# Spectral mixing and gated MLP in one kernel: two rows of x asked for ahead of a DFT block, and a row's statistics ahead of a low part on VectorE

## The chip, the cores and the metric

The kernel runs on one core of a Trainium2 chip. The metric is the device time of one execution in microseconds (us), here the median over several runs. The engines are TensorE (PE; PEld for its weight loads), VectorE (DVE), ScalarE (ACT), GpSimd (POOL) and SyncE (SP). Each takes its instructions in the order in which the program lists them for that engine. SP issues nearly all loads of the part that matters here.

## The reference

x has 2048 rows of 512 numbers. A first half mixes it by Fourier matrices, a second half is a gated MLP with a matrix over the sequence. Both are added to x, and six vectors (from a small product with `c`) scale, shift and gate them.

```python
def _A_ref(x, dft_seq_re, dft_seq_im, dft_hid_re, dft_hid_im):
    a = jnp.einsum("bsd,ed->bse", x, dft_hid_re)
    b = jnp.einsum("bsd,ed->bse", x, dft_hid_im)
    return jnp.einsum("ts,bse->bte", dft_seq_re, a) - jnp.einsum("ts,bse->bte", dft_seq_im, b)

def _B_ref(x, w_in, w_sp, b_sp, w_out):
    z = _gelu(jnp.einsum("bsd,df->bsf", x, w_in))
    z1 = z[..., :Fh]
    z2 = _layernorm(z[..., Fh:], axis=-1)
    g = jnp.einsum("ts,bsf->btf", w_sp, z2) + b_sp[None, :, None]
    return jnp.einsum("bsf,fd->bsd", z1 * g, w_out)

mod = (_silu(c) @ w_mod).reshape(c.shape[0], 6, 1, -1)
sa, ca, ga, sb, cb, gb = (mod[:, 0], mod[:, 1], mod[:, 2], mod[:, 3], mod[:, 4], mod[:, 5])
h = _layernorm(x, axis=-1) * (1 + ca) + sa
x = x + ga * _A_ref(h, ...)
h = _layernorm(x, axis=-1) * (1 + cb) + sb
return x + gb * _B_ref(h, ...)
```

The change lies in the first 40 us of the first half: layer norm of x's rows, and the product of the sequence DFT matrices with them.

## The kernel before, in words

**Numbers in two parts.** All matrix products run in fp32r. Each operand is split into a high part (an fp32r copy, made on ScalarE) and a low part (the rest, a subtraction on VectorE), and a product is three matmuls: high with high, high with low, low with high (`matmul3`, L95 to L99).

**Tiles of the DFT matrices.** The sequence matrices come in blocks of 512 by 512 (`src`, real and imaginary in turn), 1 MB each, which SP loads with four DMAs of 256 KB into one of two `stage` buffers (`load_block`, L156). I call them block 0, 1, 2, and so on; the "fourth DFT block" of the change is block 3, an imaginary one. From a block VectorE makes four tiles of 128x512 by a transpose of 32x32 squares (L191, written to `t`). From `t`, ScalarE makes the high part `ah` (L268), and VectorE the low part `al` (L286). There are two buffers for `t`, four for `ah` and three for `al`. When the last tile of a block has been transposed, the load of the block two further on is put on SP (L269 to L272 in `prep_hi`, L478 to L480 in `turn_front`).

**Rows of x.** Row s, for s from 0 to 15, is here a set of 128 of the 2048 rows, with all 512 columns. Four rows together are one buffer `x`, of which there are two; a call of `load_x` (L422) loads some of the four with four DMAs. Rows 6 and 7 (the seventh and eighth) are 512 KB: four DMAs of 128 KB, each with 32 partitions for both rows. For rows 0 to 3, `stats_first` (L436) puts three small instructions on VectorE (L439, L441, L442) and two on GpSimd (L443, L444); ScalarE makes the high part `hh` (L491) and the normed row `xn` (L121), and VectorE the low part `hl` (L533, `lo_h`). For rows 4 to 9, `stats_x` (L433) puts L105 and L107 on VectorE and three small steps on GpSimd, then `norm_x` L121, `hi_h` L528 and `lo_h` L533 follow.

**Order of the work.** The order is written by hand, and each engine keeps it. First comes a list of calls, the head (from L1095), which prepares rows 0 to 3 and tiles 0 to 6. Then a loop runs over tiles n (L1277): `prep(n)` makes the high part of tile n+3 and the low part of tile n+2 where they don't exist yet; `mm_a(n)` puts the tile's twelve matmuls on TensorE; `run(n)` makes the calls that `at(n, ...)` has put down for this n. `FRONT` (L150) says that the first eight tiles are those of blocks 0 and 1, which are multiplied with rows 0 to 3 (L551 and L557). Tiles 8 to 11 are those of block 2, multiplied with rows 4 to 7; tiles 12 to 15 are those of block 3, again with rows 4 to 7; tiles 16 to 19 are those of block 4, with rows 8 to 11. From tile 8 on the matmuls are those of L97, L98 and L99: `ah` with `hh`, `al` with `hh`, `ah` with `hl`, four times per tile.

**What stands in the rows around the change.** Statistics of rows 4 and 5 are called at n = 4, their `hl` at n = 7. Statistics of rows 6 and 7 are called at n = 6 and so stand on VectorE ahead of tile 10's transpose, of tile 9's `al`, and of the `hl` of rows 4 and 5. In the program before, rows 6 and 7 are asked for at n = 0 (L1146), when the head has already put block 2 and block 3 on SP. The program gives SP's DMAs eight semaphores in turn, and each DMA waits until the eighth before it has landed. The first DMA of a block waits besides until the last transpose from its buffer is done.

Of the kernel before, what the change touches and what calls it, by code (L numbers as in the profile page):

```python
# [20 lines left out]
def fnet_gmlp_kernel(  # L21
# [98 lines left out]
    def apply(dst, src, scale_shift):  # L120
        nc.scalar.activation(dst, src, AF.Identity, bias=scale_shift[1], scale=scale_shift[0])  # L121
# [3 lines left out]
    def at(n, f, *a):  # L125
        fill.setdefault(n, []).append((f, a))
# [39 lines left out]
    def load(b):  # L166
        if b < len(src):
            stage[b] = blocks.tile([P, 16, P], F32, tag="stage", bufs=2, name=f"stage{b}")
            load_block(stage[b], src[b])
        elif b < len(src) + 2:  # L170
            j = b - len(src)
            XB.append(blocks.tile([P, 4, Q], F32, tag="stage", bufs=2, name=f"xb{j}"))
            for g in range(2):
                nc.sync.dma_start(XB[j][:, 2 * g:2 * g + 2], ht_d[g].rearrange("(k p) t -> p k t", p=P)[:, 2 * j:2 * j + 2])
                for kk in range(2):
                    TT[2 * j + kk, g] = XB[j][:, 2 * g + kk]
        elif 4 * (b - NB0) < NE - N4:
            i, gh = divmod(b - NB0, NQ)
            g, h = divmod(gh, 2)
            p = PROD[i]  # L180
            stage[b] = blocks.tile([P, 2, 16, 64], F32, tag="stage", bufs=2, name=f"stage{b}")
            for r in range(2):
                load_half(stage[b][:, r], s_d[S_OF[p], r, g] if p in S_OF else
                          quad(w_sp, r + (2 if p == 4 else 0), g + (2 if p == 1 else 0)), h)
# [5 lines left out]
    def squares(dst, block, k):  # L190
        nc.vector.transpose(dst.rearrange("p (b i) -> p b i", i=32), block[:, :, 32 * k:32 * k + 32])  # L191
# [10 lines left out]
    def slot(i, name, dtype=F32):  # L202
        return slots[0].tile([P, Q], dtype, tag=f"slot{i}", bufs=1, name=name)
# [19 lines left out]
    def form_t(n):  # L223

        if n < N1:
            gg, p, kk = (n - N2) // 4, (n - N2) // 2 % 2, n % 2
            return TT[2 * p + kk, gg]
        p = YPROD[(n - N1) // 4 % len(YPROD)]
        gg, kk = divmod(n % 4, 2)
        a, b, c, d = TT[kk, gg], TT[2 + kk, gg], TT[kk, 2 + gg], TT[2 + kk, 2 + gg]  # L230
        return {6: S2[gg, kk], 7: a if n < N3 else c, 4: b if n < N3 else d, 5: c if n < N3 else a, 3: d if n < N3 else b}[p]
# [21 lines left out]
    def prep_hi(n):  # L253
        if n >= NE or n in highs:
            return
        highs.add(n)
        if N2 <= n < N4:
            T[n] = form_t(n)
        else:
            b, k = FRONT[n] if n < len(FRONT) else divmod(n, 4) if n < N2 else (NB0 + (n - N4) // 4, (n - N4) % 4)  # L260
            if n not in T:
                T[n] = blocks.tile([P, Q], F32, tag="t", bufs=2, name=f"t{n}")
                if n >= N4:
                    squares(T[n], stage[b][:, k % 2], k // 2)
                else:
                    squares(T[n], stage[b], k)
        AH[n] = SE[2][:, n - N4] if N4 <= n < N4 + 4 else blocks.tile([P, Q], F32R, tag="ah", bufs=4, name=f"ah{n}")
        nc.scalar.activation(AH[n], T[n], AF.Copy)  # L268
        if not N2 <= n < N4 and k == 3 and b in stage:  # L269
            stage.pop(b)  # L270
            if b != NB0:
                load(b + 2)  # L272


    def prep_lo(n):
        if n >= NE or n in lows:
            return
        lows.add(n)
        if N2 <= n < N4 and n % 4 == 3:
            AL[n] = slot(0, f"al{n}", F32R) if slots else zrow[0].tile([P, Q], F32R, tag="z1u", bufs=6, name=f"al{n}")  # L280
        elif N4 <= n < N4 + 4:
            AL[n] = slot(9 + n - N4, f"al{n}", F32R)
        else:
            AL[n] = blocks.tile([P, Q], F32R, tag="al", bufs=3, name=f"al{n}")
        t = T.pop(n)
        nc.vector.tensor_tensor(AL[n], t, AH[n].bitcast(F32), op=ALU.subtract)  # L286
# [135 lines left out]
    def load_x(g, ks=range(4), eng=nc.sync):  # L422

        if g not in XG:
            XG[g] = spool.tile([P, 4, D], F32, tag="x", bufs=2, name=f"x{g}")
        k0, k1 = ks[0], ks[-1] + 1
        v = x.rearrange("(g a k i) d -> g a i k d", g=NQ, a=4, i=32)
        for a in range(4):
            eng.dma_start(XG[g][32 * a:32 * a + 32, k0:k1, :], v[g, a][:, k0:k1, :])
        for k in ks:  # L430
            X[4 * g + k] = XG[g][:, k, :]
# [4 lines left out]
    def stats_first(s):  # L436

        m = spool.tile([P, 12], F32, tag="first", bufs=4, name=f"first{s}")
        nc.vector.bn_stats(m[:, :6], X[s])  # L439
        mv = m[:, 8:]  # L440
        nc.vector.bn_aggr(mv[:, :2], m[:, :6])  # L441
        nc.vector.tensor_scalar(mv[:, 1:2], mv[:, 1:2], EPS, None, op0=ALU.add)  # L442
        nc.gpsimd.tensor_tensor(mv[:, 2:3], mv[:, 1:2], mhalf, op=ALU.pow)  # L443
        nc.gpsimd.tensor_scalar(mv[:, 3:4], mv[:, 0:1], mv[:, 2:3], -1.0, op0=ALU.mult, op1=ALU.mult)  # L444
        NRM[s] = mv[:, 2:3], mv[:, 3:4]
# [28 lines left out]
    def turn_front(n):  # L474
        b, k = FRONT[n]
        T[n] = blocks.tile([P, Q], F32, tag="t", bufs=2, name=f"t{n}")
        squares(T[n], stage[b], k)
        if k == 3:  # L478
            stage.pop(b)
            load(b + 2)  # L480
# [7 lines left out]
    def hi_first(s):  # L488
        h_hi[s] = hpool.tile([P, ND, P], F32R, name=f"hh{s}")
        h = h_hi[s].rearrange("p k (a i) -> p k a i", i=32)  # L490
        nc.scalar.activation(h, X[s].rearrange("p (a k i) -> p k a i", a=4, i=32), AF.Identity,  # L491
                             bias=NRM[s][1], scale=NRM[s][0])
        nc.scalar.activation(h_hi[s][:, 0, :1], ones[:, :1], AF.Copy)
# [16 lines left out]
    def ones_x(s):  # L510
        LN[s] = spool.tile([P, D], F32, tag="xn", bufs=4, name=f"xn{s}")
        nc.gpsimd.memset(LN[s][:, 0:1], 1.0)

    def norm_x(s):

        if s not in LN:
            ones_x(s)
        elif s > 3:
            nc.gpsimd.memset(LN[s][:, 0:1], 1.0)
        apply(LN[s][:, 1:], X.pop(s)[:, 1:], NRM.pop(s))  # L520
# [9 lines left out]
    def lo_h(s):  # L530
        h_lo[s] = hpool.tile([P, ND, P], F32R, name=f"hl{s}")
        lo, h = parts_h(s, h_lo)
        nc.vector.tensor_tensor(lo, h, parts_h(s, h_hi)[0].bitcast(F32), op=ALU.subtract)  # L533
        LN.pop(s)
# [593 lines left out]
    stats_first(2)  # L1128
    turn_front(4)
    turn_front(5)  # L1130
    prep_hi(4)
    hi_first(2)
    prep_lo(4)
    norm_x(2)
    stats_first(3)
    lo_h(2)
    prep_hi(5)
    prep_lo(5)
# [4 lines left out]
    prep_hi(6)  # L1143
    lo_h(3)
    prep_lo(6)
    at(0, load_x, 1, range(2, 4))  # L1146
    at(2, load_row)
    at(9, silu_row)
    at(4, load_x, 2)
# [323 lines left out]
```

## Time and profile before

| what | value |
|---|---|
| median of 3 runs | 938.84 us (938.52 to 940.54) |
| the profiled execution's own time | 939.66 us |
| its span, from the first to the last instruction | 937.9 us |
| time outside the span | 1.76 us |
| TensorE busy | 925.8 us, 99% of the span |
| VectorE, ScalarE, GpSimd busy | 738.2 us (79%), 409.5 us (44%), 201.4 us (21%) |
| mean granted TensorE clock | 0.996 |
| moved by DMA | 157.88 MB, 168 GB/s on average |

How to read the rows. A row of the timeline has the start (us from the span's start), the time taken, engine, line, operation, what is written from what is read, form and count; in brackets at the end the engine's idle time before it and who ended it. Matmuls overlap, so the time from one matmul's start to the next tells the pace, not the length of one. A row of the waits has who waited, for whom, the sum, the number of times and the longest. In the chain of waits (the chain of work that ended last) a DMA's row lasts from its issue until it has landed. For a DMA, "to landing" is the time from its issue on SP until its last piece has landed. In the table by stretches, PEclk is the clock that TensorE was granted (1.00 is full), followed by DMA share and GB/s.

### The profile page before, as it was taken

The numbers are of one execution on the slowest core, as the hardware profiler recorded it, in microseconds if no ns is written. First come the engines' busy times: TensorE is split into PE (matmuls) and PEld (weight loads), VectorE is DVE, ScalarE is ACT, GpSimd is POOL, SyncE is SP. The second block draws the span as 40 slices with busy tenths as digits, with TensorE's granted clock in tenths as the row PEclk, the third lists the DMA queues.
The fourth block names the chain that finished last, engine by engine and source line by source line (L and its number), as shares of the span: only waits on it lengthen the run. The fifth ranks groups of instructions, "written<-read, shape, count | busy, mean of one in ns | idle before, by whom it ended". The sixth has DMA issues, their size and how long they took to land.

```text
span 937.9 us, 12357 instructions
## 1 busy us (share of the span) xinstructions
PE 925.8 (99%) x4053; PEld 761.8 (81%) x4053; DVE 738.2 (79%) x1217; ACT 409.5 (44%) x735; POOL 201.4 (21%) x376
## 2 busy tenths in 40 slices
PE   9799999999999999999999999999999999999998
PEld 6588888888888888888888888888888888888887
DVE  6688976789777867966659788899799889896672
ACT  5486333333222321322577968674544544331221
POOL 2232000132645256422711320332000000000000
PEclk9899999999999999999999999999999999999999
DMA  9996673866439977897373764344464556745551
GB/s 201 222 199 121 135 158 65 177 170 161 127 89 308 292 229 224 242 340 277 100 248 127 254 233 113 102 100 107 119 147 102 120 142 136 176 96 162 183 177 57
DMA packets 251200, 157.88 MB, mean 168 GB/s; under 512 B 146656, under 2 KB 218592, under 8 KB 251008
## 3 DMA queue, kind: packets, MB, share of 16 engines
q1 hardware_dynamic: 236512, 119.57, 51.9%
q0 software_dynamic: 12272, 36.86, 11.4%
q10 hardware_dynamic: 2352, 0.66, 0.3%
q8 instruction: 32, 0.52, 0.2%
q14 instruction: 32, 0.26, 0.1%
HBM read 120.33 MB, written 36.71 MB: 167 GB/s over the span
## 4 chain that ended last, share of the span: by engine, by line
PE 95%; DVE 2%; DMA 1%; SPq 1%; ACT 0%; issue 0%; POOL 0%; ACTq 0%; DVEq 0%; POOLq 0%
PE gp L99 12%; PE gp L97 12%; PE gp L98 12%; PE gw L99 9%; PE gw L97 9%; PE gw L98 9%; PE yp L99 3%; PE yp L98 3%; PE yp L97 3%; PE op L99 3%; PE op L97 3%; PE op L98 3%; PE fp L98 1%; PE fp L97 1%; PE fp L99 1%; PE z2s L98 1%
## 5 line engine op out<-in xcount | busy, mean ns | idle before, releaser
L268 ACT ACTIVATE ah<-t 128x512 fp32r<-128x512 f32 x235 | 148.3, 632 | 367.9 <-DVE t L191 254.7
L286 DVE TENSOR_TENSOR al<-t,ah 128x512 fp32r<-128x512 f32 x235 | 160.6, 683 | 59.3 <-PE gp L98 34.0
L99 PE MATMUL gp<-ah,hl 128*128 128x512 f32 x480 | 187.7, 391 | 6.2 <-DVE hl L533 6.2
L98 PE MATMUL gp<-al,hh 128*128 128x512 f32 x480 | 187.5, 391 | 0.0
L97 PE MATMUL gp<-ah,hh 128*128 128x512 f32 x480 | 187.5, 391 | 0.0
L191 DVE STREAM_TRANSPOSE t<-stage 128x512 f32<-128x512 f32 x236 | 165.4, 702 | 7.4 <-DMA stage<-in_B_w_sp_dram 2.3
L98 PE MATMUL gw<-al,bh 128*128 128x512 f32 x400 | 155.6, 389 | 0.0
L99 PE MATMUL gw<-ah,bl 128*128 128x512 f32 x384 | 149.6, 390 | 0.4 <-DVE bl L956 0.4
L97 PE MATMUL gw<-ah,bh 128*128 128x512 f32 x384 | 149.4, 389 | 0.0
L99 PEld LDWEIGHTS gp<-ah,hl 128*128 128x128 f32 x480 | 90.6, 189 | 25.4 <-DVE hl L533 6.6
L98 PEld LDWEIGHTS gp<-al,hh 128*128 128x128 f32 x480 | 90.5, 189 | 19.0 <-DVE al L286 0.2
L97 PEld LDWEIGHTS gp<-ah,hh 128*128 128x128 f32 x480 | 90.6, 189 | 18.9
L98 PEld LDWEIGHTS gw<-al,bh 128*128 128x128 f32 x400 | 75.1, 188 | 15.7
L99 PEld LDWEIGHTS gw<-ah,bl 128*128 128x128 f32 x384 | 72.1, 188 | 16.0 <-DVE bl L956 1.1
L97 PEld LDWEIGHTS gw<-ah,bh 128*128 128x128 f32 x384 | 72.1, 188 | 14.8
L928 POOL DMA_DIRECT2D s_d<-sj x64 | 35.1, 548 | 108.1 <-DVE sj L920 82.5
L97 PE MATMUL yp<-hth,gh 128*128 128x512 f32 x128 | 49.8, 389 | 0.0
L98 PE MATMUL yp<-htl,gh 128*128 128x512 f32 x128 | 49.8, 389 | 0.0
L99 PE MATMUL yp<-hth,gl 128*128 128x512 f32 x128 | 49.8, 389 | 0.0
L673 POOL DMA_DIRECT2D ht_d<-hturn x62 | 41.0, 667 | 22.6 <-DVE hturn L669 18.5
L97 PE MATMUL op<-woh,uh 128*128 128x512 f32 x110 | 42.8, 389 | 0.0
L98 PE MATMUL op<-wol,uh 128*128 128x512 f32 x110 | 42.8, 389 | 0.0
(248 smaller groups left out, 1473.5 us busy)
## 6 DMA issues: line engine op xcount, KB each, us to landing
sj<-in_B_w_sp_dram SPq DMA_DIRECT2D x32, 512.0 KB, 6.7
s_d<-sj POOLq DMA_DIRECT2D x64, 256.0 KB, 4.3
stage<-s_d SPq DMA_DIRECT2D x128, 128.0 KB, 2.9
stage<-in_A_dft_seq_re_dram SPq DMA_DIRECT2D x60, 256.0 KB, 5.1
stage<-in_A_dft_seq_im_dram SPq DMA_DIRECT2D x60, 256.0 KB, 5.6
stage<-in_B_w_sp_dram SPq DMA_DIRECT2D x88, 128.0 KB, 3.1
wm<-in_w_mod_dram SPq DMA_DIRECT2D x16, 256.0 KB, 6.1
xr<-in_A_x_dram POOLq DMA_DIRECT2D x16, 256.0 KB, 4.6
```

Source lines behind the costliest of these rows:

```text
L97: nc.tensor.matmul(acc, ah, bh, start=first, stop=False, skip_group_check=go_on)
L98: nc.tensor.matmul(acc, ah, bl, start=False, stop=False, skip_group_check=go_on)
L99: nc.tensor.matmul(acc, al, bh, start=False, stop=last, skip_group_check=go_on)
L191: nc.vector.transpose(dst.rearrange("p (b i) -> p b i", i=32), block[:, :, 32 * k:32 * k + 32])
L268: nc.scalar.activation(AH[n], T[n], AF.Copy)
L286: nc.vector.tensor_tensor(AL[n], t, AH[n].bitcast(F32), op=ALU.subtract)
L673: eng.dma_start(v[a, i], ht[32 * a:32 * a + 32].rearrange("c (b r) -> c b r", r=32))
L928: nc.gpsimd.dma_start(s_d[m, r, g][b * P:(b + 1) * P, :], a)
```

## The change

Two things are moved, and nothing is added or removed. The call that asks for rows 6 and 7 of x goes from the first step of the loop into the head, right behind the transpose of tile 5. Since that transpose puts block 2 on SP, and the transpose of tile 7 puts block 3 there, rows 6 and 7 now stand between the two. And the statistics of row 3 (the fourth row) are called ahead of the low part of tile 4 (the fifth tile); `norm_x(2)`, which has only a ScalarE instruction here, goes with it.

```diff
     stats_first(2)
     turn_front(4)
     turn_front(5)
+    load_x(1, range(2, 4))
     prep_hi(4)
     hi_first(2)
+    stats_first(3)
+    norm_x(2)
     prep_lo(4)
-    norm_x(2)
-    stats_first(3)
     lo_h(2)
     prep_hi(5)
     prep_lo(5)
@@
     prep_hi(6)
     lo_h(3)
     prep_lo(6)
-    at(0, load_x, 1, range(2, 4))
     at(2, load_row)
     at(9, silu_row)
     at(4, load_x, 2)
```

On SP, the difference between the two orders, from block 2 on (`stage_246` is block 2, `stage_278` and `stage_282` are block 3 before and now, `x_174` is the buffer of rows 4 to 7, here the DMAs of rows 6 and 7; `ccol` and `crow` are the vector `c`):

```order
 L156 DMA stage_246<-in_A_dft_seq_re_dram 32x16x128 x4
-L156 DMA stage_278<-in_A_dft_seq_im_dram 32x16x128 x4
 L429 DMA x_174<-in_A_x_dram 32x2x512 x4
+L156 DMA stage_282<-in_A_dft_seq_im_dram 32x16x128 x4
 L333 DMA ccol<-in_c_dram 128x4x1
 L335 DMA crow<-in_c_dram 128x512
```

Rows 6 and 7 stood behind block 3 and now stand ahead of it; all else on SP is as it was.

On VectorE in the head, before (`t_242` and `t_244` are tiles 4 and 5, `first_259` holds row 3's statistics, `hl_265` is the low part of row 2, `al_256` and `al_269` are the low parts of tiles 4 and 5):

```order
 L191 STREAM_TRANSPOSE t_244<-stage_143 128x512
 L286 TENSOR_TENSOR al_256<-t_242,ah_251 128x512
 L439 BN_STATS first_259<-x_138 128x6
 L441 BN_AGGR first_259<-first_259 128x2
 L442 TENSOR_SCALAR first_259<-first_259 128x1
 L533 TENSOR_TENSOR hl_265<-xn_185,hh_253 128x512
 L286 TENSOR_TENSOR al_269<-t_244,ah_267 128x512
```

The same place now (`first_260` is row 3's statistics, `al_267` tile 4's low part, `hl_269` row 2's low part, `al_273` tile 5's):

```order
 L191 STREAM_TRANSPOSE t_244<-stage_143 128x512
 L439 BN_STATS first_260<-x_138 128x6
 L441 BN_AGGR first_260<-first_260 128x2
 L442 TENSOR_SCALAR first_260<-first_260 128x1
 L286 TENSOR_TENSOR al_267<-t_242,ah_255 128x512
 L533 TENSOR_TENSOR hl_269<-xn_185,hh_257 128x512
 L286 TENSOR_TENSOR al_273<-t_244,ah_271 128x512
```

The three statistics instructions have changed places with tile 4's low part. On TensorE, ScalarE and GpSimd no instruction changes its place; only the numbers in some names do.

## The prediction

> **What bounds the kernel now.** I read the page's engine totals first, then TensorE's waits, then the timelines around the longest wait, the chain of waits, and last the landing of the DMAs.
>
> ```profile
> PE 925.8 (99%) x4053; PEld 761.8 (81%) x4053; DVE 738.2 (79%) x1217; ACT 409.5 (44%) x735; POOL 201.4 (21%) x376
> ```
>
> ```profile
> PE gp L99 <- DVE hl L533: 6.2, 1, 6.2
> ```
>
> TensorE sets the time: it is busy in all but 12 us of 937.9, and half of what is missing is one wait for a row's low part. Whatever moves TensorE's work forward there moves the end, unless a later wait takes it back. TensorE's timeline at that place, with two earlier rows and one later that the sums below need:
>
> ```profile
> 19.14 1.07 PE L557 MATMUL gp<-al,hh 128*128 128x512 f32 x4
> 21.19 1.20 PE L557 MATMUL gp<-ah,hh 128*128 128x512 f32 x4
> ...
> 29.75 0.39 PE L98 MATMUL gp<-al,hh 128*128 128x512 f32 x1
> 36.37 0.79 PE L99 MATMUL gp<-ah,hl 128*128 128x512 f32 x1 [6.22 <-DVE hl L533]
> 36.95 0.63 PE L97 MATMUL gp<-ah,hh 128*128 128x512 f32 x1
> ...
> 40.68 0.39 PE L97 MATMUL gp<-ah,hh 128*128 128x512 f32 x1
> ...
> 57.03 0.39 PE L97 MATMUL gp<-ah,hh 128*128 128x512 f32 x1
> ```
>
> At 29.75 tile 8 has had its first two matmuls; the third needs `hl` of row 4 and starts at 36.37. Tile 9 starts at 40.68 and tile 15 at 57.03, so six tiles of twelve matmuls take 16.35 us: 2.725 a tile, 0.227 a matmul. The ten matmuls from 36.37 to 40.68 took 4.31, where ten at 0.227 are 2.27. They run at half the clock:
>
> ```profile
> 30.30:33.60 3.30, 0.00 (x0) 0.00 (x0) 0.73 (x2) 0.00 (x0) 0.00 (x0) 1.00 1.10 202
> 33.80:36.30 2.50, 0.00 (x0) 0.00 (x0) 2.46 (x6) 1.07 (x2) 2.12 (x5) 0.50 1.08 220
> 40.70:48.20 7.50, 7.50 (x35) 6.19 (x34) 6.61 (x12) 3.61 (x7) 2.50 (x7) 1.00 1.21 226
> ```
>
> So the wait costs twice: 36.37 less 29.98 (29.75 and one matmul) is 6.39, and the half clock after it 4.31 - 2.27 = 2.04. Why `hl` is late shows on VectorE:
>
> ```profile
> 17.11 0.69 DVE L286 TENSOR_TENSOR al<-t,ah 128x512 fp32r<-128x512 f32 x1
> 17.72 0.69 DVE L439 BATCH_NORM_STATS2 first<-x 128x6 f32<-128x512 f32 x1
> 18.83 0.69 DVE L533 TENSOR_TENSOR hl<-xn,hh 128x512 fp32r<-128x512 f32 x1
> ...
> 25.19 0.71 DVE L191 STREAM_TRANSPOSE t<-stage 128x512 f32<-128x512 f32 x1
> ...
> 27.14 0.65 DVE L286 TENSOR_TENSOR al<-t,ah 128x512 fp32r<-128x512 f32 x1
> 32.83 0.69 DVE L105 BATCH_NORM_STATS2 bstx<-x 128x6 f32<-128x512 f32 x1 [5.04 <-DMA x<-in_A_x_dram]
> ...
> 34.45 0.68 DVE L191 STREAM_TRANSPOSE t<-stage 128x512 f32<-128x512 f32 x1
> 35.06 0.65 DVE L286 TENSOR_TENSOR al<-t,ah 128x512 fp32r<-128x512 f32 x1
> 35.63 1.28 DVE L533 TENSOR_TENSOR hl<-xn,hh 128x512 fp32r<-128x512 f32 x2
> ...
> 38.14 0.71 DVE L191 STREAM_TRANSPOSE t<-stage 128x512 f32<-128x512 f32 x1
> ```
>
> The late `hl` does not itself need rows 6 and 7. It stands on VectorE behind their statistics, which wait for their landing. From that start at 32.83 to TensorE's restart at 36.37 the queue takes 3.54. When the loads were asked for, and when they landed, is in SP's timeline, in the chain, and in the landing times of single DMAs (the last of block 2, block 3, rows 8 to 11, and block 4):
>
> ```profile
> 17.03 1.91 SPq L156 DMA_DIRECT2D stage<-in_A_dft_seq_re_dram  x4
> 21.36 2.44 SPq L156 DMA_DIRECT2D stage<-in_A_dft_seq_im_dram  x4
> ```
>
> ```profile
> 25.83 6.88 DMA x<-in_A_x_dram
> ```
>
> ```profile
> L156 SPq DMA_DIRECT2D stage<-in_A_dft_seq_re_dram x1: 492/492/492, 18.4 to 18.4; - x1
> DMA to landing us min/median/max: 6.6/6.6/6.6
> ```
>
> ```profile
> L156 SPq DMA_DIRECT2D stage<-in_A_dft_seq_im_dram x1: 1016/1016/1016, 22.8 to 22.8; - x1
> DMA to landing us min/median/max: 7.5/7.5/7.5
> ```
>
> ```profile
> L429 SPq DMA_DIRECT2D x<-in_A_x_dram x1: 339/339/339, 31.3 to 31.3; - x1
> DMA to landing us min/median/max: 7.8/7.8/7.8
> ```
>
> ```profile
> L156 SPq DMA_DIRECT2D stage<-in_A_dft_seq_re_dram x1: 1019/1019/1019, 41.4 to 41.4; - x1
> DMA to landing us min/median/max: 6.8/6.8/6.8
> ```
>
> Block 2 is in at 25.0, block 3 at 30.3, rows 6 and 7 at 25.83 + 6.88 = 32.71, rows 8 to 11 at 39.1, block 4 at 48.2: in the order of asking, with the engines moving 202 to 226 GB/s throughout. The loads are one full stream, and a load that is put forward gains only what it no longer has to stand behind.
>
> **The change part by part.**
>
> *Rows 6 and 7 go ahead of block 3.* SP is free when block 2 is asked for, at 17.03 + 1.91 = 18.94, and so asks for them 4.9 us sooner than after block 3. They land behind block 2: their own share of the stream is 32.71 - 30.3 = 2.4, so 25.0 + 2.4 = 27.4. Block 3 then lands at 32.7. VectorE cannot use that fully. Tile 8's transpose at 25.19 starts as block 2 lands and stays there; tile 7's and tile 8's low parts and tile 9's transpose follow, so the statistics can start one low part after 27.14. One low part to the next instruction is 17.72 - 17.11 = 0.61: 27.75, just behind the landing. TensorE restarts 3.54 later, at 31.29 instead of 36.37: 5.08 us gained. A wait of 31.29 - 29.98 = 1.3 remains, since block 2's landing now sets VectorE's pace.
>
> *The clock.* The first row of the table shows the clock still full 3.4 us after TensorE went idle; the second, half. A wait of 1.3 ends long before that. From rows alone the loss lies between 0 and the 2.04 of before; I take 0, since the idle stretch with a full clock is longer than the whole new wait. [...] Of the 2.04 I leave 0.1 for the first matmul after a wait, which cost 36.95 - 36.37 = 0.58 against 0.43 at that clock. So 1.94 is gained.
>
> *Block 3 lands 2.4 us later.* Tile 12's transpose is the first to need it, 38.14 - 34.45 = 3.69 behind tile 10's. Tile 10's is now 1.62 behind the statistics (34.45 - 32.83), at 29.4, so tile 12's comes at 33.1, just behind the 32.7. If it came later, tile 11's low part stands behind it; TensorE needs that at tile 11's second matmul, 40.68 + 2 x 2.725 + 0.23 - 7.0 = 39.4. Block 3 may be 5 us late at no cost.
>
> *The rest of the stream does not get faster, but TensorE does.* Block 4 still lands at 48.2, while tile 15 starts at 57.03 - 7.0 = 50.0. Tile 16's transpose stands ahead of tile 15's low part on VectorE, so that low part is there at 48.2 + 0.1 + 0.71 + 0.65 = 49.7, and is needed by 50.0 + 0.23. This hides with 0.5 to spare, and is the narrowest place; every microsecond beyond it costs one. Rows 8 to 11, at 39.1, hold up their statistics and then tile 13's low part: 39.1 + 1.62 + 0.68 + 0.65 = 42.1, needed at 40.68 + 4 x 2.725 + 0.23 - 7.0 = 44.8. That is hidden too.
>
> *Row 3's statistics ahead of tile 4's low part.* They take 18.83 - 17.72 = 1.11. Tile 4's low part starts at 18.1 to 18.2 and ends by 18.9, ahead of its matmul at 19.14. The low part of row 2 keeps its place in time. Row 3's high part comes about 0.6 us sooner, and the small wait ahead of 21.19 (0.2 us) goes. All of it lands ahead of the wait at 29.98, whose end is set by block 2 and VectorE. So neither this gain, nor a loss if the cover of 0.2 us fails, reaches the end: it is counted at 0.
>
> Sum: 5.08 + 1.94 = 7.0 us. Against the profiled execution that is 939.66 - 7.0 = 932.6; that execution lies 0.82 above the median, so the median goes from 938.84 to **931.8 us**.
>
> **The rivals.**
>
> *The clock falls all the same (0.07).* If an average over a longer stretch decides, 1.3 us of idleness could still halve it. Against it speaks the full clock through the 3.3 us without any work. Price as before, about 2.0: 933.8.
>
> *Block 4 is too late (0.06).* Its margin is 0.5 us, and a VectorE that has waited also delivers the next low parts late. If the stream loses 1 to 2 us, since a full queue is asked for sooner, 0.5 to 1.5 come back as waits at tiles 13 to 17: up to 933.5.
>
> *Rows 6 and 7 land no sooner (0.04).* If loads asked for later share the engines with them instead of queueing behind them, they finish together with block 3 at about 32.7, and nothing changes: 938.8. The landings in order of asking speak against it. [...]
>
> *Slower (0.03).* Each DMA on SP waits for the landing of the eighth before it, and that makes block 3's four now wait for block 2's; they come up to 2 us later on SP. If the stream runs dry there, everything behind it slips. TensorE feels it at tile 15, from 0.5 us of slip on. To eat the 7.0 and leave a loss of 2 us, block 4 would have to slip by 0.5 + 7.0 + 2 = 9.5 of the 23 us between 25.0 and 48.2. Then the time is 941. Against it: at 25.0 the loads of rows 6 and 7 and of block 3 are both queued, 7.7 us of work.
>
> **How the numbers follow.** The forecast, 931.8, has 0.80. A measurement of this kernel can tell about 0.2%, 1.9 us. The forecast and the first two rivals are faster by more than that: 0.93. No sooner landing is the same: 0.04. Slower: 0.03. The range begins 0.9 under the forecast: the remaining 0.1 of the half clock and the 0.8 by which the profiled execution differs from the median. It reaches to 934.2, past the clock's case, with 0.4 for the measurement. That leaves out the 0.07 of the last two cases and the tails of the first.
>
> **What would show it.** In the profile of the changed kernel TensorE's wait for `hl` is 1.2 to 1.5 us instead of 6.22. VectorE's statistics of rows 6 and 7 start at about 27.8 with next to no wait. TensorE's matmuls behind the wait follow at 0.23, tile 9 starts near 33.7, and PEclk is 1.00 throughout. Tile 16's transpose waits for block 4 and starts at about 48.3 with TensorE's tile 15 at 50.0. The forecast is wrong if the statistics still wait beyond 29, if the clock falls, if new waits for `al` show at tiles 13 to 17, or if block 4 lands later than 48.8.

## The result and the profile after

The changed kernel takes 932.11 us (median of 6 runs, 931.88 to 932.39) against 939.37 (6 runs, 938.52 to 940.54): a ratio of 0.9923, 95% interval 0.991 to 0.9936, so 7.3 us less. The forecast was 7.0 less.

The profiled execution's span is 930.5 us where it was 937.9. TensorE's waits are now these; the 6.2 for `hl` is gone from the list, and so is a small one for `bl`:

```profile
PE busyp L368 <- DVE busy L307: 1.5, 1, 1.5
PE gp L551 <- DVE t L191: 0.6, 1, 0.6
```

VectorE's timeline in the changed kernel, from tile 8's transpose on:

```profile
25.30 0.71 DVE L191 STREAM_TRANSPOSE t<-stage 128x512 f32<-128x512 f32 x1
...
27.83 0.68 DVE L105 BATCH_NORM_STATS2 bstx<-x 128x6 f32<-128x512 f32 x1
...
30.62 1.28 DVE L533 TENSOR_TENSOR hl<-xn,hh 128x512 fp32r<-128x512 f32 x2
...
33.13 0.71 DVE L191 STREAM_TRANSPOSE t<-stage 128x512 f32<-128x512 f32 x1
...
48.00 0.71 DVE L191 STREAM_TRANSPOSE t<-stage 128x512 f32<-128x512 f32 x1 [3.14 <-DMA stage<-in_A_dft_seq_re_dram]
```

The statistics of rows 6 and 7 start at 27.83 without a wait. The first `hl` is done at 30.62 + 0.69 = 31.31, where the sum had TensorE restart at 31.29. Tile 12's transpose at 33.13 does not wait for block 3. Tile 16's at 48.00 does wait for block 4, 3.14 us, as foreseen. The last DMA of rows 6 and 7 was asked for at 20.7 and took 7.0:

```profile
L429 SPq DMA_DIRECT2D x<-in_A_x_dram x1: 426/426/426, 20.7 to 20.7; - x1
DMA to landing us min/median/max: 7.0/7.0/7.0
```

It landed at 27.7, foreseen at 27.4. TensorE in the changed kernel, first the head and then tile 8:

```profile
6.74 5.62 PE L551 MATMUL gp<-t,xn 128*128 128x512 f32 x8 [0.60 <-DVE t L191]
...
31.47 0.39 PE L98 MATMUL gp<-al,hh 128*128 128x512 f32 x1
31.70 0.39 PE L99 MATMUL gp<-ah,hl 128*128 128x512 f32 x1
...
33.96 0.39 PE L97 MATMUL gp<-ah,hh 128*128 128x512 f32 x1
...
50.28 0.39 PE L97 MATMUL gp<-ah,hh 128*128 128x512 f32 x1
```

and the same place of the head in the kernel before:

```profile
6.49 3.70 PE L551 MATMUL gp<-t,xn 128*128 128x512 f32 x8 [0.35 <-ACT xn L461]
```

Here is something that the sum did not have. There is no wait at all at tile 8, because in this execution TensorE itself came 1.7 us later: its first eight matmuls of L551 took 5.62 us instead of 3.70. Looked at one by one, they start 0.86 us apart up to 10.28, and 0.43 apart from 10.90 on, which is the pace of the kernel before. The trace's record of the granted clock begins, at full, at 10.66 us here and at 6.42 in the profile of before; that it was half until then I take from the pace, 0.86 against 0.43. (The table by stretches counts the time ahead of the first record as full.) TensorE comes to tile 8's third matmul at 31.70, just behind the `hl` at 31.31. Tile 9 starts at 33.96 instead of 40.68, which is 6.72 us of the 7.4: 4.67 because the third matmul starts sooner, and 2.05 because those behind it run at the full clock (PEclk 1.00 from 31.5 to 34.0, where before had 0.50 from 36.4 to 40.4). Tile 15 starts at 50.28.

The other 0.6 us lie far behind, in the second half. TensorE in the kernel before, and in the changed one, at the same instruction:

```profile
814.76 0.50 PE L99 MATMUL gw<-ah,bl 128*128 128x512 f32 x1 [0.35 <-DVE bl L956]
```

```profile
807.52 0.39 PE L99 MATMUL gw<-ah,bl 128*128 128x512 f32 x1
```

Up to the matmul ahead of this one (814.02 and 807.29) the distance is still 6.73; behind the wait it is 7.35 (815.56 and 808.21). This wait hangs on the landing of a block of `w_sp`, and it comes and goes: of the profiles below, that of the reordered queue with early rows has it too, with 0.5 us. I do not count it to the change.

### The profile page after: what moved, and what is told of

Read it like the earlier page. It is cut to its first block, busy times and chain, and to the rows that moved or that the text cites. A ratio compares the mean times of both kernels' runs of the same rounds, so it can differ in the third digit from the quotient of the medians.

```text
span 930.5 us, 12357 instructions
## 1 busy us (share of the span) xinstructions
PE 924.9 (99%) x4053; PEld 761.2 (82%) x4053; DVE 737.1 (79%) x1217; ACT 409.1 (44%) x735; POOL 200.4 (22%) x376
## 4 chain that ended last, share of the span: by engine, by line
PE 99%; DMA 0%; ACTq 0%; DVE 0%; issue 0%; DVEq 0%
PE gp L98 12%; PE gp L99 12%; PE gp L97 12%; PE gw L99 10%; PE gw L97 10%; PE gw L98 10%; PE yp L97 3%; PE yp L99 3%; PE yp L98 3%; PE op L99 3%; PE op L97 3%; PE op L98 3%; PE gp L557 2%; PE fp L98 1%; PE fp L97 1%; PE fp L99 1%
## 5 line engine op out<-in xcount | busy, mean ns | idle before, releaser
L286 DVE TENSOR_TENSOR al<-t,ah 128x512 fp32r<-128x512 f32 x235 | 160.2, 682 | 52.6 <-PE gp L98 27.7
```

## The experiments

My theory: VectorE takes its queue in order, so rows 6 and 7 held up the low part of row 4, which did not need them; the next limits in the stream of loads are block 2 (which sets when VectorE can go on) and then block 4; and the half clock costs about 2 us of its own. The rivals: the moved statistics carry a part; TensorE needs the early landing itself; the slow matmuls have another cause than the clock; TensorE's own arrival at tile 8 is the limit.

**The load alone.** The changed kernel with the statistics put back:

```diff
-    stats_first(3)
-    norm_x(2)
     prep_lo(4)
+    norm_x(2)
+    stats_first(3)
     lo_h(2)
```

> Only rows 6 and 7 of x are asked for ahead of block 3; row 3's statistics stay behind tile 4's low part. If the whole gain comes from the load, the time is that of the changed kernel, 932.1 within 0.4, and TensorE's wait for the low part of row 4 is under 1.5 us. If the moved statistics carry a part of it, the time lies 0.5 us or more above that.

932.24 us (5 runs, 931.78 to 933.09), ratio 0.9924 (0.9911 to 0.9936). TensorE's timeline in it:

```profile
30.22 0.50 PE L97 MATMUL gp<-ah,hh 128*128 128x512 f32 x1 [0.49 <-ACT hh L528]
30.56 0.40 PE L98 MATMUL gp<-al,hh 128*128 128x512 f32 x1
32.32 0.50 PE L99 MATMUL gp<-ah,hl 128*128 128x512 f32 x1 [1.37 <-DVE hl L533]
```

The load carries the gain, and here a wait is left at tile 8, 1.37. That it is so near to the 1.3 of the sum is luck. Block 2 landed at 26.2 in this execution, 1.0 later than in the changed kernel's profile, and tile 8's transpose on VectorE waited for it:

```profile
26.27 0.71 DVE L191 STREAM_TRANSPOSE t<-stage 128x512 f32<-128x512 f32 x1 [1.25 <-DMA stage<-in_A_dft_seq_re_dram]
```

TensorE's second matmul was 0.8 later than the sum had it (30.56 against 29.75), and so the difference is nearly the same.

**The statistics alone.** The kernel before, with only these moved:

```diff
+    stats_first(3)
+    norm_x(2)
     prep_lo(4)
-    norm_x(2)
-    stats_first(3)
     lo_h(2)
```

> Only row 3's statistics are put ahead of tile 4's low part; rows 6 and 7 are asked for behind block 3 as before. If what is gained ahead of the long wait is swallowed by it, the time is that of the kernel before, 939.4 within 0.5, with a wait of 6 to 6.6 us at tile 8. If an earlier row 3 is worth something, it is 0.2 to 0.6 us faster.

939.68 us (11 runs), ratio 1.0003 (0.9994 to 1.0012): nothing. TensorE's timeline and, from the table by stretches, its clock:

```profile
29.55 0.39 PE L98 MATMUL gp<-al,hh 128*128 128x512 f32 x1
36.21 0.79 PE L99 MATMUL gp<-ah,hl 128*128 128x512 f32 x1 [6.27 <-DVE hl L533]
```

```profile
36.30:42.00 5.70, 5.70 (x14) 4.44 (x15) 3.84 (x7) 3.60 (x8) 0.59 (x4) 0.50 1.23 239
```

TensorE is 0.2 us earlier at tile 8 and waits for it. The half clock lasted longer here than in the profile of before: about 14 matmuls instead of 10.

**The queue instead of the load.** The kernel before with its loads untouched, and the statistics of rows 6 and 7 one step later:

```diff
         m = n + (s == 9)
-        at(n, stats_x, s)
-        at(m + 1, norm_x, s)
+        late = s in (6, 7)
+        at(n + late, stats_x, s)
+        at(m + 1 + late, norm_x, s)
```

> The kernel before with its loads untouched; the statistics of rows 6 and 7 are called one step later, and so stand on VectorE behind tile 9's low part and the low parts of rows 4 and 5. If the place in VectorE's queue is what made TensorE wait, tile 8 no longer waits, and a wait of about 2.3 us for row 6's own low part comes at tile 10 instead; the clock stays full; 933.5, between 932.5 and 935. If TensorE needs the early landing itself, nothing is gained: 939.4 or more, with 6 us of wait at tile 8 or 10.

935.8 us (5 runs, 934.6 to 936.25), ratio 0.9959 (0.9944 to 0.9973): a gain of 3.7, less than I expected but not nothing. Its VectorE, TensorE and clock:

```profile
29.25 1.29 DVE L533 TENSOR_TENSOR hl<-xn,hh 128x512 fp32r<-128x512 f32 x2
33.13 0.69 DVE L105 BATCH_NORM_STATS2 bstx<-x 128x6 f32<-128x512 f32 x1 [2.59 <-DMA x<-in_A_x_dram]
```

```profile
30.06 0.43 PE L99 MATMUL gp<-ah,hl 128*128 128x512 f32 x1
...
38.21 0.50 PE L97 MATMUL gp<-ah,hh 128*128 128x512 f32 x1 [2.90 <-ACT hh L528]
```

```profile
35.40:38.10 2.70, 0.00 (x0) 0.00 (x0) 1.89 (x4) 1.91 (x4) 1.94 (x5) 1.00 1.14 211
38.30:39.80 1.50, 1.50 (x6) 0.94 (x7) 0.76 (x2) 1.41 (x3) 0.00 (x0) 1.00 1.24 228
40.00:43.20 3.20, 3.20 (x9) 2.51 (x8) 3.13 (x8) 1.35 (x4) 0.70 (x2) 0.50 1.24 222
```

The rows land as late as before, and tile 8 no longer waits: the place in the queue did it. A shorter wait, 2.90, now comes where row 6 is really needed, at tile 10. And the clock fell behind this wait too, which I had ruled out: the eight matmuls from 40.00 on start 0.43 apart instead of 0.23, about 1.6 us. With the wait 0.6 longer than the 2.3 expected, that makes up the 2.3 us by which the time lies above the expected 933.5.

**The clock alone.** The kernel before, with matmuls of ones by zeros inside the long wait (they add zeros to a running sum):

```diff
         prep(n)
+        if n == 8:
+            for _ in range(11):
+                nc.tensor.matmul(GP[0, 0, 0], ones, busy, start=False, stop=False)
         mm_a(n)
         run(n)
+        if n == 5:
+            nc.gpsimd.memset(busy, 0.0)
```

> The kernel before, with eleven matmuls of ones by zeros (they add nothing to the sum) put ahead of tile 8, 4.7 us at full clock, inside the long wait. TensorE restarts at the same time, but has been idle for at most 1.7 us. If the half clock behind the wait costs 2.0 us of its own, the time is 937.4 (939.4 - 2.0), within 0.5, and PEclk stays 1.00. If the slow matmuls behind the wait come from late operands and not from the clock, it stays at 939.4.

940.16 us (11 runs), ratio 1.001 (1.0001 to 1.0018). This one missed, by my sizing. In its timeline on TensorE

```profile
29.51 9.60 PE L1281 MATMUL gp<-busy,ones 128*128 128x512 f32 x22
38.55 0.80 PE L97 MATMUL gp<-ah,hh 128*128 128x512 f32 x1
```

the eleven stand as 22 instructions, which take 9.0 us and overrun the wait. It decides nothing. With six instead of eleven:

> The kernel before, with six matmuls of ones by zeros put ahead of tile 8, inside the long wait. Each is two passes of 0.41 us, so they take 4.9 us (the eleven of the first try took 9.0 and overran the wait by 2). TensorE is idle for 1.5 us at most and restarts at the same time as before. If the half clock costs 2.0 us of its own, 937.4 within 0.6, with PEclk at 1.00 throughout; if the slow matmuls behind the wait have another cause, 939.4.

937.22 us (11 runs, 936.59 to 937.37), ratio 0.9974 (0.9965 to 0.9983). TensorE:

```profile
29.41 5.31 PE L1281 MATMUL gp<-busy,ones 128*128 128x512 f32 x12
34.16 0.79 PE L97 MATMUL gp<-ah,hh 128*128 128x512 f32 x1
34.80 0.40 PE L98 MATMUL gp<-al,hh 128*128 128x512 f32 x1
36.56 0.50 PE L99 MATMUL gp<-ah,hl 128*128 128x512 f32 x1 [1.37 <-DVE hl L533]
```

The needed `hl` is no earlier (36.56 against 36.37), and yet 2.4 us are gained with work that is of no use (939.64 for before on this chip). Behind the wait the clock is full, and tile 9 starts at 38.95 instead of 40.68:

```profile
36.60:41.00 4.40, 4.40 (x20) 3.64 (x21) 4.37 (x8) 3.68 (x8) 0.64 (x4) 1.00 1.24 225
```

```profile
38.95 0.39 PE L97 MATMUL gp<-ah,hh 128*128 128x512 f32 x1
```

That is 1.7 us, or 1.9 counted from the restart. The other 0.6 between the two profiles is the wait at 814, which this execution does not have. The half clock is a cost of its own, of about 1.9 us.

**Still earlier, ahead of block 2.** The changed kernel, with rows 6 and 7 asked for right behind rows 4 and 5:

```diff
     load_x(1, range(2))
+    load_x(1, range(2, 4))
     keep_busy(2, 5)
...
     turn_front(5)
-    load_x(1, range(2, 4))
```

> Rows 6 and 7 of x are asked for still earlier, ahead of block 2, right behind rows 4 and 5. If VectorE's queue, which starts anew when block 2 lands, sets TensorE's restart, block 2 lands 2.4 us later (27.5), and the low part of row 4 is ready 2.4 us later, near 33.7: a wait of 2 to 4 us at tile 8, and 934.4, or up to 2 us more if that wait is long enough for the clock to fall as it did behind the wait of 2.9 us with the statistics moved back. If TensorE's own arrival at tile 8 is the limit, as the changed kernel's profile suggests (no wait at all), it stays at 932.1.

933.96 us (5 runs, 933.38 to 934.05), ratio 0.9935 (0.9922 to 0.9947): 1.8 slower than the changed kernel. Tile 8's transpose on VectorE and the restart on TensorE:

```profile
27.09 0.71 DVE L191 STREAM_TRANSPOSE t<-stage 128x512 f32<-128x512 f32 x1 [2.25 <-DMA stage<-in_A_dft_seq_re_dram]
```

```profile
33.13 0.50 PE L99 MATMUL gp<-ah,hl 128*128 128x512 f32 x1 [1.37 <-DVE hl L533]
```

Tile 8's transpose comes 1.8 us later than in the changed kernel, and so does the end. Block 2 lands at 27.0 here and sets the pace; TensorE's own arrival does not.

**Block 4 pushed back.** The changed kernel with 1 MB more ahead of block 4:

```diff
-    at(12, load_columns, 0)
+    at(5, load_columns, 0)
```

> The changed kernel, with 1 MB more ahead of block 4 in the stream: the columns of the modulation matrix that are asked for at n = 12 are asked for at n = 5. If block 4 is the next thing that bounds TensorE, it lands 4.6 us later, at 52.5; tile 15's low part is ready near 53.9 where 50.5 is needed: a wait of 3.4 us at tile 15, and 935.5, or up to 2 us more if the clock falls. If there is more room than the sum says, it stays at 932.1.

938.82 us (11 runs, 937.84 to 940.18), ratio 0.9994 (0.9985 to 1.0003). Nearly the whole gain is lost again. VectorE, TensorE's waits, and the clock:

```profile
53.12 0.71 DVE L191 STREAM_TRANSPOSE t<-stage 128x512 f32<-128x512 f32 x1 [8.84 <-DMA stage<-in_A_dft_seq_re_dram]
```

```profile
PE gp L98 <- DVE al L286: 4.2, 1, 4.2
```

```profile
55.50:58.70 3.20, 3.20 (x9) 2.48 (x8) 3.17 (x7) 3.11 (x8) 1.50 (x4) 0.50 1.24 236
```

Tile 16's transpose waits, tile 15's low part behind it is 4.2 us late, and the clock falls on top. So block 4 is the next limit, as the sum had it. The loss, 6.7 us, is larger than expected (3.4, or up to 5.4 with the clock). The wait is 4.2 us where 3.4 was expected, and the profile, at 938.1, shows one of the better runs: three with a mean granted clock of 0.998 took 937.84 to 938.45, and six with 0.996, so with more time at half clock, 938.82 to 940.18.

**Both cures together, and block 4 first.** The changed kernel with the reordered statistics of the queue experiment; then the same, and besides block 4 ahead of the first columns of `w_mod`:

```diff
-    at(5, load_columns, 1)
+    at(8, load_columns, 1)
...
-    for j, ns in ((1, (12, 14, 17, 18)), (0, (21, 22, 23, 24))):
+    for j, ns in ((1, (14, 15, 17, 18)), (0, (21, 22, 23, 24))):
```

> The changed kernel, with the statistics of rows 6 and 7 behind the low parts of rows 4 and 5 on VectorE. If VectorE's queue still holds TensorE up at tile 8, the low part of row 4 is there at about 30.0 instead of 31.3, no wait is left at tile 8, and at most 0.4 us comes at tile 10; the gain is at most 1.3 and is cut to 0.4 to 0.9 by block 4, which lands at 48 and lets tile 15's low part be ready at 49.3 to 49.7: 931.5, between 930.8 and 932.2. If TensorE's own arrival is the limit, 932.1.

> The changed kernel with the statistics of rows 6 and 7 behind the low parts of rows 4 and 5, and besides with block 4 asked for ahead of the first columns of the modulation matrix, whose first use is put off from n = 12 to n = 14 (and the second from 14 to 15). Block 4 lands 4.6 us sooner, near 43.4. If the wait of 0.6 at tile 15 was what took that order's gain back, no wait is left there, TensorE's own arrival is the limit, and the time is 0.3 to 1.5 below the changed kernel's: 931.2, with a wider spread, as TensorE's arrival at tile 8 has differed by up to 1.7 us from one profile to the next. If something else takes it back, 932.1.

> The changed kernel itself on the same chip, to compare with: 932.1 within 0.4, whatever TensorE's arrival at tile 8 is; if it arrives early (before 30.0), a wait of 1 to 1.5 us for the low part of row 4, if late (after 31), none, and tile 9 starts at 33.5 to 34.0 in both cases.

The first has 932.28 us (4 runs, 931.52 to 933.49), ratio 0.9919 (0.9906 to 0.9933): no gain over the changed kernel that can be told, where 0.6 was expected. In TensorE's waits

```profile
PE gp L98 <- DVE al L286: 0.6, 1, 0.6
PE gp L551 <- DVE t L191: 0.6, 1, 0.6
PE gw L99 <- DVE bl L956: 0.5, 1, 0.5
PE gp L97 <- ACT hh L528: 0.3, 1, 0.3
```

the wait at tile 8 is gone, and block 4 takes 0.6 back at tile 15. With block 4 first that wait is gone as well; this list is complete but for the first wait at the start of the program:

```profile
PE gp L551 <- ACT xn L461: 0.3, 1, 0.3
PE gp L97 <- ACT hh L528: 0.2, 1, 0.2
```

It has 931.53 us (5 runs, 931.29 to 932.4), ratio 0.9919 (0.9907 to 0.9931), beside 932.17 (5 runs, 931.83 to 932.48), ratio 0.9924 (0.9912 to 0.9937), for the changed kernel on the same chip. Its median is the lowest, by 0.6, but the intervals overlap; whether it beats the changed kernel stays open. In the changed kernel's second profile TensorE came early to tile 8:

```profile
29.71 0.39 PE L98 MATMUL gp<-al,hh 128*128 128x512 f32 x1
30.89 0.50 PE L99 MATMUL gp<-ah,hl 128*128 128x512 f32 x1 [0.78 <-DVE hl L533]
...
49.61 0.39 PE L97 MATMUL gp<-ah,hh 128*128 128x512 f32 x1
50.05 0.50 PE L98 MATMUL gp<-al,hh 128*128 128x512 f32 x1
```

It waits 0.78 there, less than the 1 to 1.5 expected, and 0.2 more at tile 15's second matmul, which stands 0.44 behind the first instead of 0.23. The time is the same as with the late arrival. On VectorE, tile 8's transpose comes straight behind row 5's statistics:

```profile
24.65 0.18 DVE L107 BATCH_NORM_AGGREGATE mvx<-bstx 128x2 f32<-128x6 f32 x1
24.83 0.71 DVE L191 STREAM_TRANSPOSE t<-stage 128x512 f32<-128x512 f32 x1
```

Block 2 had been in since 24.4, so it was not block 2 that VectorE waited for here.

## Why the prediction was right, point by point

**Landing and queue: right, with one limit too few.** Rows 6 and 7 landed at 27.7 and 26.5 in the two profiles of the changed kernel (foreseen 27.4), their statistics started at 27.83 and 27.37 (27.75), the `hl` was there at 31.31 and 30.84 (for a restart at 31.29). That it is a matter of VectorE's queue is shown by the experiment that reordered only the queue. The sum named block 2's landing as what sets VectorE's pace from then on. A later block 2 does (it landed at 26.2 with the load alone and at 27.0 with the load ahead of it, and tile 8's transpose waited for it). In the changed kernel it had landed at 25.2 and 24.4, and VectorE was busy until about then with the statistics of rows 4 and 5: two limits lie side by side, and the sum had one.

**The wait left over: right in kind, its size partly luck.** The sum took TensorE's arrival at 29.98 for fixed. It was 31.70 in one profile of the changed kernel and before 30 in the other. An early TensorE waits for `hl` (0.78), a late one comes just behind it; tile 9 starts at 33.29 and at 33.96. The early one loses 0.2 at tile 15 and 0.3 more near 102 us, and the two executions took the same 932.32. That step of the sum had the right end for an incomplete reason. The late arrival comes from the head: the first eight matmuls of L551 began at 6.74 and took 5.62 us in the one profile, and began at 6.41 and took 4.19 in the other. Both are profiles of the changed kernel, so it is not the change that makes it late.

**The clock's 1.94: right, measured at 1.9 with the clock kept up through the long wait**, and at 2.05 between the profiles of before and after. But the reason why it would not fall behind a short wait was too strong. I argued that a wait shorter than the 3.4 us which the clock had once survived was safe. The queue experiment contradicts it: 2.90 us of waiting, a PEclk of 1.00 for the first 1.5 us of work behind it (38.3 to 39.8), and then 0.50 (40.0 to 43.2). Behind waits of 0.78 and 1.37 the matmuls went on 0.23 to 0.24 apart from the second on, so the forecast stood, but not for the reason given against the rival that the clock falls all the same.

**Block 3 late at no cost: right.** Tile 12's transpose came at 33.13 and 33.04 (foreseen 33.1); in the second profile it waited 0.41 us for block 3, and TensorE did not feel it. The last DMA of block 3 was asked for at 25.2 instead of 22.8, as the rival of a slower stream had it, but the block was in at 32.5 (foreseen 32.7): the stream did not run dry. **Block 4 as the narrowest place: right.** Its transpose came at 48.00 and 48.71 in the changed kernel's two profiles, where 48.3 was foreseen; tile 15 started at 50.28 and 49.61. Asked for behind 1 MB more, it came at 53.12, and that cost 6.7 us.

**Row 3's statistics: right, 0.** The experiment with these alone lies within a tenth of a per cent of the kernel before.

**The 0.6 us at 814** were in neither term; they come from a wait that some executions have and others not. The agreement of the totals, 7.3 against 7.0, is therefore in part luck.

## What to carry to other kernels

A wait is to be priced with its place in the queue: look at what the waiting engine has behind the stalled instruction, not only at who reads the late data. Here the loads were one stream of 202 to 226 GB/s, and putting one forward paid by about what it passed (a block of 5.3 us, from 25.0 to 30.3; the rows landed 5.0 and 6.2 us sooner). The loads that it passes have margins of their own, which have to be worked out one by one at the new, earlier pace. The longer waits on TensorE cost more than their length here, through the clock: 2.0 us behind a wait of 6.2, and 1.6 behind one of 2.9.

## What the runs showed of the hardware that I had not expected

The clock fell behind a wait of only 2.90 us, about 1.7 us after TensorE had gone back to work. The stretch at half clock was not of one length: some 9 matmuls behind that wait, 10 in the profile of before, 14 in the one with the statistics alone. By PEclk and the pace of the matmuls (0.43 us apart at half clock, 0.23 at full) it ran from about 39.9 to 43.3 behind that wait, and from about 55.4 to 58.8 with block 4 pushed back, 3.4 us each. The trace of before has it from 33.72 to 40.55, 6.8 us. With the statistics alone PEclk is 0.50 from 32.2 on and the slow pace ends near 42.2: 10.0 us or more.

Nor did the clock fall at one distance from the start of the wait: 3.6 us behind it in the profile of before (from 30.15), at most 2.3 with the statistics alone (from 29.94), both with TensorE still idle; but 4.6 in the queue experiment (from 35.31), and 5.2 with block 4 pushed back (from 50.23), where TensorE had waited 4.2 us and been back at work for 0.9. What decides when the clock falls, and for how long, is open. The slow start differs from one execution to the next too, as the 5.62 and 4.19 us of the first eight matmuls of L551 show.

The kernel before spreads widely: 937.83 to 940.92 in 15 runs of one chip, against 936.59 to 937.37 in 11 runs with the clock kept full (mean granted clock 1.0 in each) and 931.83 to 932.48 in 5 of the changed kernel. A longer stretch at half clock goes with a longer time: three of the 15 runs had a mean granted clock of 0.994 or 0.995 and took 939.89 to 940.92. But the other twelve all had 0.996 and took 937.83 to 940.49, so most of the spread has another cause, which is open.
